# A new order table for the engines of an attention and feed-forward kernel

## The chip, the cores and the metric

The kernel runs on one core of a Trainium2 chip. A core has four engines that compute, each with its own list of instructions that it works off in order: TensorE (PE in the profile; its weight loads are PEld), VectorE (DVE), ScalarE (ACT) and GpSimd (POOL). SyncE (SP) only issues transfers. The metric is device microseconds (us) of one execution, as the median of several runs.

## The reference

Two layers in a row. The first is attention through 32 memory slots per head, for 8 batches, 8 heads, 576 tokens, 64 elements per head. The second is a feed-forward layer on 4608 tokens, 512 wide inside and outside and 2048 wide in the middle:

```
a      = softmax(phi, over tokens)               # 8 x 8 x 576 x 32
k_m    = a^T k ;  v_m = a^T v                    # 32 x 64 per head
attn   = softmax(q k_m^T / 8, over the 32 slots)
x      = attn v_m, heads side by side            # 4608 x 512
h      = x w_in                                  # 4608 x 2048
out    = (h * cos(h)) w_out                      # 4608 x 512
```

All inputs and outputs are fp32, but for w_in and w_out, which arrive as 64-bit floats and are brought to fp32 on the chip.

## The kernel before

**The work.** x is never formed. As x w_in = attn (v_m w_in), the kernel multiplies the 32 x 64 memories of a batch by w_in (a *fold*: tiles pv and vw, lines 641 to 687), and the attention weights aT by that (first product, tile hp, line 718). For batch 0 and 1 a fold is in fp32 (line 659, tiles pvf and pv), for the later ones in pairs of fp16 numbers (lines 645 and 650). hp is turned into h cos(h) by six steps that alternate between ScalarE and VectorE: lines 729 (ACT), 730 (DVE), 735 (ACT, Sin), 739 (DVE), 741 (ACT) and 742 (DVE); the result is gp, again a pair of fp16 numbers. The second product (line 760) multiplies gp by w_out (tile wo) into acc. In group 0 both products are fp32 (lines 709 and 755), and gp ends at line 737.

**Tiling.** The 4608 rows are 12 groups of 384, a group has three acc tiles of 128 rows, and 16 steps f over the middle dimension: 192 steps (grp, f) in all. While group 0 runs, the eight parts of w_in and the eight of w_out are loaded into three buffers (raw0 to raw2, `load_w_in` and `load_w_out`), brought to fp32 (`to_float32`: cast line 257, shift and or line 260, Square line 263, whose end frees the buffer), and split into fp16 pairs in group 1 (lines 303 to 315). The memories of a batch (psA, line 460), its scores (sc, line 562) and its folds are made some way ahead of the groups that use them.

**Tile sizes on TensorE.** A matmul uses the 128 x 128 array whole (lines 709, 718, 755, 760, 812), or a part: 128 x 32 (most of line 460, and line 645) or 64 x 32 (lines 562, 650, 659). Small matmuls on different parts can run beside each other. An fp32 product is two hardware matmuls in the trace, so a fold at line 659, written as 8 matmuls, is 16 of the trace.

**Buffers.** Three banks hold hp, two hold small results (pv, psA, sc and others in turn), three hold acc.

**The order.** The program is written as loops that emit all instructions in a program order. Then `issue_in_order` (last line of `attention_then_ffn`) sets, for every engine, the order in which it issues them, from the table `NEXT`. A word of the table is a position in what is left of the engine's program-order list, and `xN` repeats it: `0x26` takes the first one 26 times, `8` takes the one that then stands eight places behind the front. An engine waits at an instruction until its operands are there, and all behind it waits too. The waits themselves follow from the data, whatever the order. 43 matmuls of zeros (line 812, "warm") fill TensorE's time while the first inputs arrive.

Of the kernel before, what the change touches and what calls it, by code (L numbers as in the profile page):

```python
# [49 lines left out]
        "0x16 2x2 0x16 1x8 0x10 1x8 0 1x8 0x8 1 0x2 1 0x50 2 3 4 5 0x4 8 0x2 7 8 0x6 5x2 0x2 1 0x2 16x2 26x2 "  # L50
        "0 79 65x2 77 1 0x6 70 0 1 2 0x3 1 0x3 80 79 58 0 1 2 3 54 0x4 66 67 66 0x40 34x3 36x2 34 0x2 32x2 0 "
        "1 0x4 1 0 24x2 0x8 18 19 0x2 27 1 0 1 0 1 0 10 8x2 16x2 0x3 1 0 1 0x2 8x2 18 16x2 17 16 18x2 16x2 "
        "0x6 1 0 11 8 0x2 1 0 1 0x2 1x3 0x5 1 0x4 2x2 0x2 4 0x4 1x2 0 1 0 14 1x13 0 22 0x2 1 0x4 1 0 27 0x12 "
        "2x12 1 2x13 0x4 13x3 0 12x3 0x12 3x2 4 5 3x2 4 3x16 0x3 6x12 3x3 9x3 0x3 24x3 0x3 15x3 0x3 12x3 0x24 "
        "6x3 0x7 19x3 1 0x2 1 0x15 6x12 0x3 6x3 0x3 6x12 0x3 3x3 0x3 18x3 3x3 18x3 0x30 3x3 6x12 9x3 0x6 3x3 "
        "0x3 20x3 0x14 3x3 0x3 40x5 0x41 6x3 0x3 3 0x5 8x3 0x12 1 2 0 2 0x9 17x6 6x4 7 6x2 7 8 6x2 3x3 0x9 "
        "3x6 12x6 3x3 0x6 6x3 0x3 3x3 15x3 12x2 73x2 0x3 9 0x6 12x6 0x3 6x3 15x6 0x6 6x3 0x6 12x3 6x6 0x18 "
        "9x3 0x9 3x3 0x12 3x3 0x13 1 0 1 0 1 0 40x9 0x40 8x6 3x5 20x6 0x3 6x3 3x3 0x7 1 0 1 0x4 3x3 17x3 3 4 "
        "5 3 5 3x3 0x3 9x3 0x6 3x4 27x3 0x8 1 2 3 0x4 6x3 0x6 9x3 0x3 6x3 15x3 0x15 3x9 0x6 6x8 0x3 3 4 3 4 5 "
        "3 14x3 5x9 0x3 11 0x5 6x8 0x6 6x3 18x3 6x6 0x27 1 0x2 1 2 0x8 6x3 0x3 3x6 9x3 3x3 0x12 3x3 0x3 3x10 "  # L60
        "4 3 4 5 3x8 6x3 3x3 0x3 3x6 0x3 6x3 3x3 12x3 3x6 0x3 15x3 3x3 15x9 16 17 15x2 16 15x2 3x6 9x12 0x3 "
        "3x3 0x24 3x6 0x21 15x3 0x3 18x8 0x12 14x15 6 7 6x2 7 6x3 0x6 46x12 0x3 43x3 0x3 46x15 43x3 40x3 0x40 "
        "8x7 13x3 6 7x5 0x6 1x3 0 27 3x4 7 8 9 10 0x11 8x11 0 1 2 3 4x3 0x4 3x3 29x3 3 4 3 4 3x2 4 3x13 0x3 "
        "3x3 21x3 18x3 3x12 0x3 18x3 0x15 21x3 6x12 0x3 3x3 0x3 18x3 3x12 0x3 3x3 0x3 18x3 0x15 3x15 0x3 3x3 "
        "0x9 3x3 0x3 9x3 21x3 0x3 6x6 12x3 0x6 18x3 6x3 0x6 6x3 0x18 28x3 0x3 3x9 4 3 4 3 4 3x2 0x3 9x3 21x3 "
        "6x3 0x15 3x9 0x3 3x9 0x20 1 2 0 2 0x2 1 0 6x3 9x3 0x9 12x3 9x3 0x6 12x3 3x6 0x3 6x6 3x3 0x3 9x8 3x3 "
        "6x3 7 6 7 6x2 0x3 43x6 54x6 0x3 43x3 0x43 5x2 12x3 6x3 9 5 3x2 8x3 0x6 5x3 0x5 14x3 0x2 1 2 0x2 1 "
        "0x7 3x11 0x5 1 0 1 0x3 8x9 0 1 2 3 0x4 3x9 9x9 0x6 3x3 6x3 0x15 12x2 0x3 10x3 0x9 1x3 0x10 6x6 3x3 "
        "0x6 3x3 0 14x3 8x3 0x8 3x6 0x3 6x3 3x3 15x3 0x9 3x9 0x3 3x3 0x3 3x8 4 3 4 3 4 3x9 0x6 3x3 9x3 45x4 "
        "3x6 15x3 0x18 9x3 3x9 0x3 3x6 4 3x5 0x3 18x3 0x12 3x15 0x3 9x12 3x3 0x3 6x3 3x3 0x6 12x3 0x26 1 2 "  # L70
        "0x2 1 0x3 12x6 0x15 40x12 46x3 40x3 55x3 40x15 0x43 5x15 3x5 6x4 10 11 12 13 0x6 16 0x8 8x14 11x3 0 "
        "1 2 3 0x7 26x3 0x2 1 0x3 1 0 12x3 27x3 0x15 15x3 0x15 12x9 0x27 3x3 0x3 18x3 0x12 3x3 0x3 15x6 0x15 "
        "96x4 12x9 0x18 3x12 0x3 3x3 15x3 0x3 9x3 42x4 0x9 3x9 0x3 3x3 0x3 6x3 0x9 3x2 4 3x5 0x3 12x3 0x6 6x6 "
        "0x3 3x3 39x4 9x6 18x6 0x6 6x3 0x6 24x6 6x3 0x6 3x5 4 5 3x5 0x3 3x3 0x3 3x6 0x3 3x3 6x6 3x3 0x3 6x3 "
        "0x3 18x8 9x3 12x3 0x3 63x3 9 10 9 10 9x4 0x49 20x2 9x3 0x6 5x6 12x3 0x3 6x3 3x6 9x3 0x10 1 2 0x3 1 "
        "0x7 24 0x8 1 2 3 0 3 0x2 17x2 0 8x5 12x3 8x3 0x2 1 2 0x2 1 0x2 9x3 6x3 0x18 6x9 3x3 6x3 0x6 6x3 18x2 "
        "6x3 16x3 15 6x3 0x12 9x4 3x6 0x3 11x3 0x2 21x3 9x3 0x9 9x3 0x3 39x8 0x9 9x3 6x6 12x3 15x3 0x6 23x3 "
        "9x2 10 9 10 11 9x2 0x6 21x3 12x3 0x9 3x6 15x3 0x9 9x3 0x6 15x3 9x3 0x3 9x13 10 9x2 0x6 3x12 0x6 3x3 "
        "0x3 15x6 12x3 27x3 0x12 33x3 0x12 3x3 0x3 12x3 46x3 12x3 0x28 12x3 0x15 12x6 0x12 15x3 33x3 15x3 "
        "30x3 0x3 12x3 58x3 0x24 31x3 0x13 1 0 1 0x3 30x3 27x3 0x12 30x3 3x12 0x6 15x3 12x3 24x3 42x3 0x12 "  # L80
        "12x3 27x3 0x15 27x3 0x12 33x3 0x15 3x3 18x3 3x12 24x3 0x6 30x3 0x15 9x3 3x6 18x3 0x18 12x3 24x3 6x3 "
        "33x3 0x6 9x3 0x3 6x3 24x3 0x12 12x3 21x3 33x3 12x3 6x12 30x3 6x6 12x3 6x9 24x3 6x6 9x3 18x3 0x3 3x9 "
        "18x3 30x3 6x6 3x3 6x3 30x3 15x3 24x3 3x3 33x3 9x3 3x12 15x3 3x3 0x3 21x3 0x6 12x3 0x18 3x3 0x3 6x3 "
        "0x3 9x3 3x3 0x3 3x3 0x9 3x6 9x3 6x3 0x9 "),
    mybir.EngineType.Activation: (
# [897 lines left out]
```

## Time and profile before

| | |
|---|---|
| median of 3 runs | 691.31 us (691.0 to 692.96) |
| the profiled execution's own time | 690.88 us |
| its span, first to last instruction | 689.1 us |
| TensorE busy | 676.9 us (98%) |
| VectorE busy | 524.1 us (76%) |
| ScalarE busy | 499.3 us (72%) |
| mean granted TensorE clock | 0.997 |

The span lies inside the execution's time; 1.8 us lie around it. Matmuls are pipelined and their ends in the trace are modelled: a matmul's duration runs on while the next has started, and "busy" is the union of these. What a stretch of TensorE work costs is therefore read from the starts of its rows. In the timeline a row is one or more like instructions: start, length, engine, line, operation, tiles, form and count; what stands in brackets is the engine's idle time before it, and what ended that.

### The profile page before, as it was taken

What the parts mean: (1) busy time and instruction counts of PE and PEld (TensorE: products, weight loads), DVE (VectorE), ACT (ScalarE), POOL (GpSimd) and SP (SyncE); (2) the same over time, 40 slices, a digit from 0 to 9 for tenths busy, and PEclk for the clock granted to TensorE, in tenths of its full rate; (3) what the DMA queues carried; (4) which work ended last, traced back from release to release, by engine and by line L of the source; (5) the groups of instructions that cost most, each with busy time, mean ns of one, the idle gap of its engine ahead of it and who ended that gap; (6) DMA issues with size and microseconds to landing.
All of it is one profiled execution on the core that took longest, in us unless ns stands there. A gap on an engine that the chain in (4) does not pass through costs nothing.

```text
span 689.1 us, 12262 instructions
## 1 busy us (share of the span) xinstructions
PE 676.9 (98%) x4815; PEld 346.7 (50%) x4815; DVE 524.1 (76%) x1117; ACT 499.3 (72%) x934; POOL 20.0 (3%) x26
## 2 busy tenths in 40 slices
PE   8899999999999999999999999999999999999997
PEld 3343446564554445555444445655445445665553
DVE  6789999999879765797668965798657876566643
ACT  2698999988788865779665965778746856665653
POOL 4020000000000000000000000000000000000000
PEclk9999999999999999999999999999999999999999
DMA  8997784337043000620105300350100000100001
GB/s 294 381 336 260 296 267 120 87 70 265 16 148 111 31 1 1 217 73 0 47 2 174 114 1 1 116 174 0 47 1 2 15 32 1 47 1 1 16 30 47
DMA packets 28521, 66.21 MB, mean 96 GB/s; under 512 B 2288, under 2 KB 12400, under 8 KB 26416
## 3 DMA queue, kind: packets, MB, share of 16 engines
q1 hardware_dynamic: 24000, 57.43, 25.2%
q10 hardware_dynamic: 4464, 8.00, 3.1%
q8 instruction: 38, 0.62, 0.4%
q14 instruction: 19, 0.16, 0.1%
HBM read 51.79 MB, written 9.44 MB: 89 GB/s over the span
## 4 chain that ended last, share of the span: by engine, by line
PE 87%; DVE 5%; ACT 3%; DMA 2%; issue 1%; SPq 0%; ACTq 0%
PE acc L760 46%; PE hp L718 24%; PE acc L755 5%; PE hp L709 3%; PE psA L460 3%; PE pv L645 2%; DMA raw_in<-in_w_in 2%; PE sc L562 1%; PE pv L650 1%; PE pvf L659 1%; DVE u L730 1%; DMA kv<-in_k_first 1%; ACT gp L729 1%; DVE u L739 1%; PE pv L659 1%
## 5 line engine op out<-in xcount | busy, mean ns | idle before, releaser
L760 PE MATMUL acc<-wo,gp 128*128 128x512 f16 x1584 | 373.4, 379 | 0.2 <-ACT gp L741 0.2
L760 PEld LDWEIGHTS <-gp 128*128 128x128 f16 x1584 | 151.1, 98 | 168.2 <-issue 11.5
L718 PE MATMUL hp<-aT,vw 128*128 128x192 f16 (+1 forms) x1440 | 199.1, 284 | 0.9 <-DVE u L739 0.5
L718 PEld LDWEIGHTS <-vw 128*128 128x128 f16 x1440 | 129.0, 98 | 71.6 <-issue 10.9
L729 ACT ACTIVATE gp<-hp,cu 128x192 int32<-128x192 f32 (+1 forms) x240 | 114.4, 490 | 48.8 <-PE hp L718 32.9
L730 DVE SCALAR_TENSOR_TENSOR u<-hp,cu,gp 128x192 f32<-128x192 f32 (+1 forms) x240 | 117.8, 502 | 40.5 <-ACT gp L729 39.6
L735 ACT ACTIVATE u<-u,quarter 128x384 f32<-128x384 f32 x192 | 115.7, 612 | 44.3 <-DVE u L730 42.7
L739 DVE SCALAR_TENSOR_TENSOR u<-hp,u 128x384 f32<-128x384 f32 x176 | 96.2, 552 | 46.7 <-ACT u L735 45.9
L742 DVE TENSOR_TENSOR gp<-u,gp 128x384 f16<-128x384 f32 x176 | 96.0, 551 | 31.5 <-ACT gp L741 30.5
L741 ACT CAST gp<-u 128x384 f16<-128x384 f32 x176 | 87.9, 507 | 38.4 <-DVE u L739 35.7
L755 PE MATMUL acc<-wo,gp 128*128 128x512 f32 x96 | 46.6, 605 | 0.2 <-DVE gp L737 0.2
L666 DVE SCALAR_TENSOR_TENSOR vw<-pv,vw 128x512 f16<-128x512 f32 x48 | 32.3, 684 | 14.2 <-ACT vw L665 14.2
L665 ACT ACTIVATE vw<-pv 128x512 f16<-128x512 f32 x48 | 27.1, 591 | 8.6 <-PE pv L650 8.4
L755 PEld LDWEIGHTS acc<-wo,gp 128*128 128x128 f32 x96 | 16.9, 190 | 18.8 <-issue 15.2
L784 ACT ACTIVATE ob<-acc,os 128x512 f32<-128x512 f32 x27 | 18.2, 686 | 11.2 <-PE acc L760 10.4
L709 PE MATMUL hp<-aT,vf 128*128 128x384 f32 x64 | 24.2, 499 | 0.2 <-DVE gp L737 0.2
L735 ACT ACT_TABLE_LOAD x17 | 21.8, 1283 | 0.3
L460 PE MATMUL psA<-kv,phi 128*32 128x129 f32 (+1 forms) x560 | 17.8, 275 | 0.0
L709 PEld LDWEIGHTS hp<-aT,vf 128*128 128x128 f32 x64 | 11.5, 189 | 12.2 <-issue 4.8
L460 PEld LDWEIGHTS psA<-kv,phi 128*32 128x32 f32 (+1 forms) x560 | 14.5, 109 | 4.1 <-issue 2.2
L562 PE MATMUL sc<-q,km 64*32 64x288 f32 (+2 forms) x256 | 14.1, 414 | 1.2 <-DVE om L795 0.5
L812 PE MATMUL warm<-zeros 128*128 128x512 f16 x43 | 14.0, 468 | 1.2 <-DVE vmask L173 1.2
(157 smaller groups left out, 486.4 us busy)
## 6 DMA issues: line engine op xcount, KB each, us to landing
kv<-in_kv SPq DMA_DIRECT2D x28, 516.0 KB, 6.4
raw_out<-in_w_out SPq DMA_DIRECT2D x8, 1024.0 KB, 6.4
q<-in_qT SPq DMA_DIRECT2D x7, 1152.0 KB, 5.6
out<-ob ACTq DMA_DIRECT2D x30, 256.0 KB, 2.1
raw_in<-in_w_in SPq DMA_DIRECT2D x6, 1024.0 KB, 7.9
phi<-in_phi SPq DMA_DIRECT2D x8, 512.0 KB, 5.7
w_in_sb<-w_in_parts SPq DMA_DIRECT2D x12, 256.0 KB, 4.3
wo<-in_w_in SPq DMA_DIRECT2D x2, 1024.0 KB, 13.9
```

What stands on the lines that cost most here:

```text
L460: nc.tensor.matmul(psA[32 * j:32 * (j + 1), g * KV:(g + 1) * KV], lhsT=a[:n, c, h * M:(h + 1) * M], rhs=kvs[c][:n, h * KV:(h + 1) * KV], s ...
L666: nc.vector.scalar_tensor_tensor(out=vw[:, 1, g], in0=src, scalar=T, in1=vw[:, 0, g], op0=ALU.mult, op1=ALU.subtract)
L709: nc.tensor.matmul(hp[:, :GT], lhsT=st["vf", q][:, g, fo * P:(fo + 1) * P], rhs=st["aTf"][:, g], start=(g == 0), stop=(g == 1))
L718: nc.tensor.matmul(hp[:, c0:c0 + n], lhsT=vw[:, wi, g, fo * P:(fo + 1) * P], rhs=aT[:, ai, g, c1:c1 + n], start=(k == 0), stop=(k == 5))
L729: nc.scalar.activation(ni[:, c], hp[:, c], AF.Copy, scale=cu, bias=0.25)
L730: nc.vector.scalar_tensor_tensor(out=u[:, c], in0=hp[:, c], scalar=cu, in1=ni[:, c], op0=ALU.mult, op1=ALU.subtract)
L735: nc.scalar.activation(u, u, AF.Sin, scale=TWO_PI_BELOW, bias=quarter)
L739: nc.vector.scalar_tensor_tensor(out=u, in0=hp[:, :GT], scalar=2.0 ** -17, in1=u, op0=ALU.mult, op1=ALU.mult)
L741: nc.scalar.copy(gp[:, 0], u)
L742: nc.vector.tensor_tensor(out=gp[:, 1], in0=u, in1=gp[:, 0], op=ALU.subtract)
L755: nc.tensor.matmul(accs[grp][t], lhsT=gp[:, t * P:(t + 1) * P], rhs=wo[:, f + 1], start=(f == 0), stop=(f == NF - 1))
L760: nc.tensor.matmul(accs[grp][t], lhsT=gp[:, gi, t * P:(t + 1) * P], rhs=parts[:, wi], start=(f == 0 and gi == 0 and wi == 0), stop=(f == N ...
```

## The change

Only the table `NEXT` is changed. The instructions, their operands and their number are the same (4143 matmuls as written, 915 instructions of ScalarE, 1117 of VectorE, 22 of POOL, 112 of SP); SP's list is the same word for word. 3828, 838, 1079 and 11 of the first four stand at another place of their engine's list, half of TensorE's by 9 places or fewer. The diff, cut to the first lines of each engine:

```diff
 NEXT = {
     mybir.EngineType.PE: (
-        "0x16 2x2 0x16 1x8 0x10 1x8 0 1x8 0x8 1 0x2 1 0x50 2 3 4 5 0x4 8 0x2 7 8 0x6 5x2 0x2 1 0x2 16x2 26x2 "
-        "0 79 65x2 77 1 0x6 70 0 1 2 0x3 1 0x3 80 79 58 0 1 2 3 54 0x4 66 67 66 0x40 34x3 36x2 34 0x2 32x2 0 "
...
+        "0x26 8 0x16 1x8 2x8 0 2x8 5x3 0x2 4 5 3x2 4 3x2 7x24 9x16 0x3 6x2 8 9 10 0x4 4x2 5 4x2 0x4 6 7 8 6x3 "
+        "0x6 1 0x3 16 27x2 16 0 1 2 0x5 72 58x2 0 1 2 0x3 1 0 62 60 0x2 59 58 74x2 75 0 1 2 3 0x4 67 0x40 "
...
     mybir.EngineType.Activation: (
-        "0x6 4 0 3 0x4 2 3 0 1 5 8 1 9 12 4 8 1 0 8 4 2 0 9 1 8 2 10 0x2 3 0 12 2 15 5 10 0x3 10 0 3 6 1 5 0 "
...
+        "0x4 1x3 3x2 1x2 0 1 4 2x2 6 0 2 4 9 12 6 8 10 1 4 12 3 1 3 13x2 3 0 16 5 2 18 2x2 3 2 14 10 0 1 0x2 "
...
     mybir.EngineType.DVE: (
-        "0 5 0 5 4 0 1 2x2 1x7 0x5 1 0x4 6x3 0 5 0x2 7 3 0 2 1x2 0x2 1 2 0x2 1 0 13 15 11 15 11 0 19 1 0 17 0 "
...
+        "0 7 8x3 0 7x9 5 6 7x2 13 2 12 5 4 10x2 14 9x3 4 8x6 3 8 7 18 1 18 6 16 7 19 25 17 18 15x2 6 20 6x2 "
...
     mybir.EngineType.Pool: (
-        "0x22 "),
+        "2 0 3 2 1 0 1x2 0x5 1 0x8 "),
     mybir.EngineType.SP: (
         "0x35 5 0x3 2 0x13 12 1 0x8 1 0x2 2x2 0x6 2x2 0x6 2x2 0x6 2x2 0x6 2x2 0x12 "),
 }
```

What the unrolled lists hold for TensorE, where a *run* is a stretch of small tiles between two whole ones, and a *piece* is a stretch of one line's matmuls:

| | before | after |
|---|---|---|
| changes of tile size, whole list | 199 | 167 |
| changes of tile size from the first pvf_2 product on | 179 | 148 |
| runs of small tiles from there on | 77 | 58 |
| of these psA (line 460) | 7 | 7 |
| sc (line 562) | 16 | 15 |
| pvf and pv in fp32 (line 659), 10 folds | 15 | 10 |
| pv in fp16 pairs (lines 645 and 650), 24 folds | 39 | 26 |
| pieces of line 645, and of line 650 | 30, 28 | 26, 26 |
| runs that end in an fp32 tile of line 709 or 755 | 16 | 12 |

On POOL the clearings of w_in_sb and wo come in another order, and the first two clearings of wo by line 270 stand ahead of the first all-reduce (l3_0), behind which they stood. On VectorE two of the three clearings of w_in_sb (line 189) stand behind the start of the first batch's maximum, and the use of l3_0 (line 277) stands later.

148 rows, old and new, of the table NEXT are left out of this document.

## Prediction

> **What bounds the kernel now.** I read the page first: its busy line, then the chain of waits, then the costliest group.
>
> ```profile
> span 689.1 us, 12262 instructions
> PE 676.9 (98%) x4815; PEld 346.7 (50%) x4815; DVE 524.1 (76%) x1117; ACT 499.3 (72%) x934; POOL 20.0 (3%) x26
> ...
> PE 87%; DVE 5%; ACT 3%; DMA 2%; issue 1%; SPq 0%; ACTq 0%
> ...
> L760 PE MATMUL acc<-wo,gp 128*128 128x512 f16 x1584 | 373.4, 379 | 0.2 <-ACT gp L741 0.2
> ```
>
> TensorE is busy nearly throughout and makes up 87% of the chain. The mean of 379 ns is a duration from start to modelled end, and matmuls overlap; what one costs the stream is the distance between starts. For that I read TensorE's timeline (first number: start; second: duration).
>
> ```profile
> 208.25 0.71 PE L562 MATMUL sc<-q,km 64*32 64x288 f32 x16
> 208.90 1.47 PE L760 MATMUL acc<-wo,gp 128*128 128x512 f16 x6
> 210.21 1.14 PE L718 MATMUL hp<-aT,vw 128*128 128x384 f16 x6
> 211.27 0.40 PE L645 MATMUL pv<-w_in_sb,vp 128*32 128x512 f16 x4
> 211.60 1.47 PE L760 MATMUL acc<-wo,gp 128*128 128x512 f16 x6
> 213.00 0.40 PE L645 MATMUL pv<-w_in_sb,vp 128*32 128x512 f16 x4
> 213.33 0.41 PE L650 MATMUL pv<-w_in_sb,vl 64*32 64x512 f16 x8
> 213.68 0.82 PE L760 MATMUL acc<-wo,gp 128*128 128x512 f16 x3
> 214.33 1.14 PE L718 MATMUL hp<-aT,vw 128*128 128x384 f16 x6
> 215.31 2.75 PE L760 MATMUL acc<-wo,gp 128*128 128x512 f16 x12
> 217.90 1.14 PE L718 MATMUL hp<-aT,vw 128*128 128x384 f16 x6
> ```
>
> Twelve L760 matmuls take 217.90 - 215.31 = 2.59 us, 0.216 each. Six that are followed by a small tile take 213.00 - 211.60 = 1.40, where 6 x 0.216 is 1.30: **entering a small tile size costs 0.10 us**. The stream shows no gap here, and still time goes: into entering small tiles, and into short pieces of small tiles, which cost almost as much as long ones (below).
>
> Then the busy time by stage: startup, group 0, group 1, groups 2 to 10 (columns: length; busy time of PE, PEld, DVE, ACT, POOL; clock; DMA). The bounds are the first L755 or L760 matmul of each group.
>
> ```profile
> 0.00:33.40 33.40, 27.61 (x275) 11.13 (x275) 22.85 (x48) 13.49 (x23) 8.51 (x11) 0.95 0.96 335
> 33.40:111.70 78.30, 77.44 (x455) 35.49 (x456) 71.49 (x151) 73.16 (x123) 4.66 (x5) 1.00 0.77 269
> 111.70:169.40 57.70, 57.44 (x474) 32.67 (x473) 54.67 (x119) 52.32 (x105) 0.35 (x1) 1.00 0.50 138
> 169.40:640.20 470.80, 469.15 (x3387) 245.24 (x3385) 350.06 (x755) 335.46 (x641) 6.45 (x9) 1.00 0.16 52
> ```
>
> TensorE's idle time after 33.4 us is 0.86 + 0.26 + 1.65 = 2.8 us. So from group 0 on the end is set by how much stream time TensorE's own list takes. But in groups 0 and 1 VectorE and ScalarE are nearly full too: VectorE idles 6.8 + 3.0 = 9.8 us of 136, ScalarE 5.1 + 5.4. There a worse order of theirs would show at once. From 169 us on they have a quarter of the time free.
>
> **The change part by part.** No instruction is added or removed; Sin and Exp alternate equally often in both ScalarE lists, so the activation table loads stay 34. SP's list is the same. I unrolled both lists of each engine and compared.
>
> *TensorE, from the first pvf_2 product on.* The same 161 instructions stand ahead of that point in both lists, so the rest is the same work: 179 changes of tile size before, 148 after; 77 runs of small tiles before, 58 after. Prices of pieces, from starts again:
>
> ```profile
> 41.60 0.81 PE L709 MATMUL hp<-aT,vf 128*128 128x384 f32 x2
> 42.34 0.64 PE L659 MATMUL pvf<-w_in_sb,vm 64*32 64x256 f32 x8
> 42.91 0.91 PE L709 MATMUL hp<-aT,vf 128*128 128x384 f32 x2
> ...
> 82.16 0.62 PE L659 MATMUL pvf<-w_in_sb,vm 64*32 64x256 f32 x2
> 82.71 1.12 PE L755 MATMUL acc<-wo,gp 128*128 128x512 f32 x2
> ...
> 128.82 1.04 PE L659 MATMUL pv<-w_in_sb,vm 64*32 64x512 f32 x2
> 129.79 0.82 PE L760 MATMUL acc<-wo,gp 128*128 128x512 f16 x3
> ...
> 271.01 0.61 PE L645 MATMUL pv<-w_in_sb,vp 128*32 128x512 f16 x8
> 271.56 2.15 PE L718 MATMUL hp<-aT,vw 128*128 128x192 f16 x24
> ```
>
> - L659 with 256 columns: two hardware matmuls (one fp32 product) hold the stream 0.55 us, eight hold it 0.57. A piece costs 0.55 whatever is in it. Pieces 10 to 6: 4 x 0.55 = **2.2 us**.
> - L659 with 512 columns: one product alone holds 0.97. Pieces 5 to 4: **1.0 us**.
> - L645 and L650, the 24 folds: four L645 hold 0.33 and eight hold 0.55, so a fold cut in two pays 2 x 0.33 - 0.55 = 0.11; the L650 part holds 213.68 - 213.33 = 0.35. Pieces of L645 30 to 26: 4 x 0.11 = 0.4; of L650 28 to 26: 2 x 0.35 = 0.7. **1.1 us**.
> - L562: 16 runs become 15. A whole set holds 0.65. The row of a half was not free of waits, so I bound it: a half cannot cost less than half a set (saving 0) nor more than a whole (saving 0.65). I take 0.6, since in the nearest rows, L659's, a piece costs nearly the whole.
> - Entering: 19 runs fewer x 0.10 = **1.9 us**.
> - Leaving into an fp32 tile: two L709 hold 41.60 to 42.34, drawn with 0.81, but 0.91 behind pvf: 0.10 more. Such exits 16 to 12: **0.4 us**.
>
> Sum: 2.2 + 1.0 + 1.1 + 0.6 + 1.9 + 0.4 = **7.2 us** of stream taken off. In this measure gp_1_15's first use, near the end of group 1, comes 3.7 us earlier.
>
> [...]
>
> *TensorE's first 161 instructions (startup).* The warm matmuls stand as 14, 2, 7, 1, 2, 3, 4, 4, 6 in place of 14, 8, 2, 1, 4, 4, 2, 2, 6, and VectorE does one clearing of w_in_sb ahead of the maximum and two later, in place of three early. TensorE idles 5.8 us in this stage and the clock mean of 0.95 is worth 0.05 x 33.4 = 1.7 us. What sets this stage are loads and conversions in a chain; SP issues the same loads in the same order. Bounds: a gain of 1.7 if the slow stretch of clock goes away, a loss of 1.7 if a second one comes. I take 0, as both lists reach gp_0_0 with nearly the same VectorE work ahead of it (22.7 and 22.0 us).
>
> *VectorE and ScalarE in groups 0 and 1.* Here a loss could hide. For every gp tile I added up the durations of all VectorE instructions that stand in its list ahead of the tile's last step (L737 or L742), and the stream time of all TensorE instructions ahead of its first use, in both lists. The margin after is the margin seen now, less the VectorE work put ahead, plus the TensorE work put ahead. The largest shift is at gp_1_0:
>
> ```profile
> 103.73 0.55 DVE L742 TENSOR_TENSOR gp<-u,gp 128x384 f16<-128x384 f32 x1
> ...
> 111.65 0.81 PE L760 MATMUL acc<-wo,gp 128*128 128x512 f16 x3
> ```
>
> Now it is ready at 104.28 and used at 111.65: 7.4 us. VectorE's list has 5.5 us more ahead of it, TensorE's 0.6 less: 1.3 left. Over the 32 tiles of both groups none falls below zero; the least is 0.6 (gp_1_8). This holds if VectorE idles no more than its present 9.8 us. The same sum for vf, vw and the converted weights gives 0.7 or more wherever groups 0 and 1 read them. In groups 3 to 10 the TensorE work between an hp tile and its gp's first use has a shortest value of 8.9 us, where it was 6.3, so waits there should not grow. New waits net of old ones: from -2.8 (all present idle goes) to +9.8 (VectorE's idle doubles and all of it lands); I take **+1.1**, the idle that TensorE shows in groups 0 and 1 now, once more.
>
> *POOL.* The all-reduce for l3_0 moves behind two clearings of wo that wait for ScalarE. Its reader on VectorE moves back by more (from 16.0 to 56.5 us of VectorE work), so nobody stands behind it: 0. If VectorE came early it would wait for ScalarE's Squares of parts 2 and 3 of w_in, within the +9.8.
>
> *The tail.* Both lists end with acc_11_2's matmuls and the same evacuation: 0, or some tenths more since acc_11_0 and acc_11_1 end nearer to the end.
>
> Sum against the profiled execution's own 690.88 us: 690.88 - 7.2 + 1.1 = 684.8. The median of the runs, 691.31, lies 0.43 above that execution, so I forecast **685.2 us** for a median.
>
> **The rivals.**
> - *VectorE and ScalarE cap groups 0 and 1.* TensorE's 3.7 us there turn into waits: 685.2 + 3.7 = 688.9. For it: 6.8 and 3.0 us of idle only. Against: the margins stay positive.
> - *A late weight load.* ScalarE's Square frees the buffer of raw_out_0 for the load of raw_in_4.
>
> ```profile
> 37.61 1.06 ACT L263 ACTIVATE raw_out<-wo 128x1024 f32<-128x1024 f32 x1
> ...
> 54.85 1.35 ACT L257 CAST w_in_sb<-raw_in 128x1024 f16<-128x1024 bf16 x1
> DMA to landing us min/median/max: 4.8/7.9/12.3
> ```
>
>  Of the 16 us between them 14.9 are ScalarE work now, 6.8 in the new list, less than the median landing of raw_in (7.9; the last row, from the view of that tile). At worst 12.3 - 6.8 = 5.5 us late on a nearly full engine: 690.7. Against: seven other such pairs stand only 5.8 to 7.9 us of ScalarE work apart now.
> - *The pieces filled idle time*, so that the change doesn't shorten what matters: 691. Against: the stream shows 2.8 us of idle, less than 7.2.
> - *Slower.* VectorE's list stands in worse step with ScalarE's in groups 0 and 1, each waiting for the other in order, and its idle doubles by 9.8 us. Past the margin at gp_1_0 each us of it delays TensorE: 685.2 + 9.8 - 1.3 = 693.7. It outweighs the gain from some 8 us of extra idle on. For it: 93% full, and an order made with mean durations.
> - *TensorE has room after all.* If its matmuls could follow each other faster than the list shows, it would be held by others and a shorter list would change nothing: 691.3. Twelve in 2.59 us without a gap speak against it. [...]
>
> **How the numbers follow.** Some 0.3% (2.1 us) is what a measurement of this kernel can tell from no change. The forecast (682.3 to 688): 0.67. VectorE's cap 0.12, half of it beyond 689.2; late load 0.05, two fifths faster; idle filled 0.08, same; slower 0.07; TensorE with room 0.01, same. Faster 0.67 + 0.06 + 0.02 = 0.75; same 0.06 + 0.03 + 0.08 + 0.01 = 0.18; slower 0.07. The range goes from 682.3 (the old waits gone too) to 690.5, which takes in the cap and most of the late load.
>
> **What would show it.** Right: folds as L645 x8 and L650 x8 in one piece, about 0.89 us from start to the next large tile; L659 in whole groups; the first L755 at 33 +- 2 us; gaps of TensorE after it of some 4 us at the most; first use of gp_2_0 2 to 3 us earlier than 169.4. Wrong: idle of TensorE that ends on L737, L742 or L666 in groups 0 and 1, VectorE idling over 12 us there, or ScalarE waiting for raw_in between 45 and 60 us.

## The result, and the profile after

The changed kernel takes 684.97 us (median of 5 runs, 684.13 to 687.55) where the kernel before takes 691.31 (690.64 to 692.96): a ratio of 0.9912 with a 95% interval of 0.9886 to 0.9937. The forecast was 685.2 us, in a range of 682.3 to 690.5. The profiled execution took 684.29 us.

Lines of the changed kernel stand 4 further down: L764 is the old L760, L759 the old L755, L722 the old L718, L663 the old L659, L649 and L654 the old L645 and L650. In the kernels of the experiments the lines are shifted by a few in the same way; the tiles tell which is meant. First the page: busy line, chain, costliest group.

```profile
span 682.5 us, 12301 instructions
PE 670.8 (98%) x4815; PEld 347.3 (51%) x4815; DVE 518.7 (76%) x1117; ACT 494.1 (72%) x934; POOL 20.7 (3%) x26
...
PE 74%; DVE 11%; ACT 10%; DMA 2%; issue 2%; SPq 0%; ACTq 0%; DVEq 0%
...
L764 PE MATMUL acc<-wo,gp 128*128 128x512 f16 x1584 | 373.4, 379 | 0.3 <-DVE gp L746 0.2
```

The counts of the engines' own work and the mean of 379 ns are the old ones. What is new is the chain: TensorE 74% where it was 87%, VectorE and ScalarE 21% where they were 8%. More of the end now hangs on a tile that TensorE takes up the moment it is ready. The stages, in the same bounds of time as before:

```profile
0.00:33.40 33.40, 27.78 (x291) 11.88 (x292) 23.01 (x43) 12.90 (x21) 8.16 (x10) 1.00 0.96 336
33.40:111.70 78.30, 78.30 (x490) 37.90 (x489) 74.16 (x161) 77.19 (x135) 5.95 (x6) 1.00 0.78 268
111.70:169.40 57.70, 57.70 (x458) 32.99 (x457) 55.03 (x119) 52.81 (x102) 0.35 (x1) 1.00 0.28 69
169.40:640.20 470.80, 468.38 (x3389) 245.72 (x3388) 346.87 (x758) 331.83 (x643) 6.23 (x9) 1.00 0.18 60
```

Three things are to be seen. The clock of the startup is 1.00 where it was 0.95. Between 33.4 and 169.4 us TensorE has no idle time at all (1.1 us before), VectorE has 6.8 us (9.8 before) and ScalarE 6.0 (10.5). The changed kernel does some of group 2 in this time; in its own groups 0 and 1, from 32.79 to 161.94 us, VectorE idles 6.4 us and ScalarE 5.8. Behind 169.4 TensorE idles 2.4 us, more than the 1.65 of before. The folds and their surroundings on TensorE's timeline:

```profile
32.19 0.67 PE L663 MATMUL pvf<-w_in_sb,vm 64*32 64x256 f32 x16
32.79 1.12 PE L759 MATMUL acc<-wo,gp 128*128 128x512 f32 x2
...
208.93 0.61 PE L649 MATMUL pv<-w_in_sb,vp 128*32 128x512 f16 x8
209.48 0.41 PE L654 MATMUL pv<-w_in_sb,vl 64*32 64x512 f16 x8
209.82 2.76 PE L764 MATMUL acc<-wo,gp 128*128 128x512 f16 x12
212.42 1.14 PE L722 MATMUL hp<-aT,vw 128*128 128x384 f16 x6
```

A fold stands in one piece and takes 209.82 - 208.93 = 0.89 us. Twelve output matmuls still take 2.60 us, 0.216 each.

The profiled executions differ by 6.59 us: the first output matmul starts 0.64 us earlier (32.79 for 33.43), from there to the last matmul's end it is 646.04 us where it was 652.02 (5.98 less), and the rest up to the end of the span is the same (3.67 for 3.66).

This last measure, **from the first output matmul to the last matmul's end**, is used in all that follows. It is much sharper than the run's time: in two executions of the changed kernel the starts of the output matmuls, counted from the first one, agreed within 0.03 us at each of 27 places over the 646 us. It is still one execution, and one accident has to be known. At 330 us of the kernel before, ScalarE issues two output transfers, which took 1.46 us; in e_warm_before, whose lists are the same there, they took 0.92:

```profile
329.74 1.46 ACTq L786 DMA_DIRECT2D out<-ob  x2
...
334.46 1.63 PE L760 MATMUL acc<-wo,gp 128*128 128x512 f16 x6 [0.15 <-ACT gp L741]
```

```profile
330.26 0.92 ACTq L781 DMA_DIRECT2D out<-ob  x2
```

The first rows are of the kernel before, the last of e_warm_before. ScalarE's next steps came later for it, gp_5_2 was late, and the output matmuls waited 0.47 us at 334 us; e_warm_before has no wait there and is 0.45 us shorter at just this place. So some 0.45 of the 5.98 us belongs to that execution and not to the order. The table below is worked out from the starts of TensorE's matmuls. "Runs" are stretches of small tiles behind 32 us and "their time" goes from their start to the next large tile. "Waits" are distances between large matmuls beyond 0.216, 0.163 and 0.083 us (512, 384 and 192 columns in 16 bits), 0.429, 0.323 and 0.110 (fp32; 512, 384 and 128 columns), and 0.093 more into a small tile, each where it is over 15 ns.

```
kernel         runs  their time  waits 32-170  waits behind 170  first output to last  median of the runs (kernel before beside it)
before          77      63.9         3.2            2.5               652.0             691.31
after           58      59.0         1.5            4.9               646.0             684.97  (691.31)
after_again     58      59.0         1.5            4.9               646.0             684.26  (691.99)
e_join          56      64.3         6.5            2.6               653.0             692.85  (692.27)
e_join_late     64      63.2         3.5            3.4               650.8             691.44  (691.99)
e_cutB          78      65.5         1.7            5.0               654.7             693.94  (692.27)
e_cutAB         78      60.2         2.0            5.8               650.5             690.21  (692.27)
e_start         58      59.0         3.1            5.0               646.2             687.36  (692.27)
e_pool          57      58.7         1.5            4.9               646.4             684.43  (691.99)
e_repair        58      59.2         1.5            5.5               646.9             686.82  (691.99)
e_warm          58      59.0         1.7            4.9               646.1             684.19  (692.06)
e_warm_before   77      63.9         3.5            2.1               651.6             690.24  (692.06)
e_best          56      59.0         1.5            5.0               645.8             684.48  (692.06)
e_swap          58      59.0         1.5            4.2               645.4             683.44  (692.30)
```

The measured 5.98 us are the 4.9 of the shorter runs and 1.8 for 19 entries at 0.093, less 0.7 of new waits. Most of it comes early. Both lists have the same large matmuls ahead of the first use of gp_3_0, and there (222.77 us before, 216.96 after) the changed kernel is already 5.2 us ahead, counted from the first output matmul. Behind it the runs of small tiles go on to get shorter, but new waits of 2.0 us leave only 0.8.

### The profile page after: what moved, and what is told of

Read it like the earlier page. It is cut to its first block, busy times and chain, and to the rows that moved or that the text cites. A ratio compares the mean times of both kernels' runs of the same rounds, so it can differ in the third digit from the quotient of the medians.

```text
span 682.5 us, 12301 instructions
## 1 busy us (share of the span) xinstructions
PE 670.8 (98%) x4815; PEld 347.3 (51%) x4815; DVE 518.7 (76%) x1117; ACT 494.1 (72%) x934; POOL 20.7 (3%) x26
## 4 chain that ended last, share of the span: by engine, by line
PE 74%; DVE 11%; ACT 10%; DMA 2%; issue 2%; SPq 0%; ACTq 0%; DVEq 0%
PE acc L764 37%; PE hp L722 19%; PE acc L759 6%; PE hp L713 3%; DVE u L734 2%; ACT u L739 2%; PE psA L464 2%; ACT gp L733 2%; DVE u L743 2%; DVE gp L746 2%; DMA kv<-in_v_first 1%; PE pv L649 1%; ACT gp L745 1%; PE sc L566 1%; PE pv L654 1%
## 5 line engine op out<-in xcount | busy, mean ns | idle before, releaser
L764 PE MATMUL acc<-wo,gp 128*128 128x512 f16 x1584 | 373.4, 379 | 0.3 <-DVE gp L746 0.2
L764 PEld LDWEIGHTS <-gp 128*128 128x128 f16 x1584 | 151.1, 98 | 169.5 <-issue 11.3
L722 PE MATMUL hp<-aT,vw 128*128 128x192 f16 (+1 forms) x1440 | 199.9, 283 | 1.7 <-DVE u L743 0.8
L722 PEld LDWEIGHTS <-vw 128*128 128x128 f16 x1440 | 130.0, 98 | 73.6 <-issue 10.0
L733 ACT ACTIVATE gp<-hp,cu 128x192 int32<-128x192 f32 (+1 forms) x240 | 115.8, 492 | 68.0 <-PE hp L722 36.1
L759 PE MATMUL acc<-wo,gp 128*128 128x512 f32 x96 | 45.9, 604 | 0.0
L759 PEld LDWEIGHTS acc<-wo,gp 128*128 128x128 f32 x96 | 16.9, 190 | 19.0 <-issue 16.9
L713 PE MATMUL hp<-aT,vf 128*128 128x384 f32 x64 | 22.7, 491 | 0.0
L464 PE MATMUL psA<-kv,phi 128*32 128x129 f32 (+1 forms) x560 | 17.9, 275 | 0.1
L572 DVE STREAM_TRANSPOSE at<-sc 128x288 f32<-128x288 f32 (+2 forms) x32 | 14.2, 464 | 1.2 <-PE sc L566 1.2
```

The lines of the kernel that those rows point to most:

```text
L464: nc.tensor.matmul(psA[32 * j:32 * (j + 1), g * KV:(g + 1) * KV], lhsT=a[:n, c, h * M:(h + 1) * M], rhs=kvs[c][:n, h * KV:(h + 1) * KV], s ...
L713: nc.tensor.matmul(hp[:, :GT], lhsT=st["vf", q][:, g, fo * P:(fo + 1) * P], rhs=st["aTf"][:, g], start=(g == 0), stop=(g == 1))
L722: nc.tensor.matmul(hp[:, c0:c0 + n], lhsT=vw[:, wi, g, fo * P:(fo + 1) * P], rhs=aT[:, ai, g, c1:c1 + n], start=(k == 0), stop=(k == 5))
L733: nc.scalar.activation(ni[:, c], hp[:, c], AF.Copy, scale=cu, bias=0.25)
L759: nc.tensor.matmul(accs[grp][t], lhsT=gp[:, t * P:(t + 1) * P], rhs=wo[:, f + 1], start=(f == 0), stop=(f == NF - 1))
L764: nc.tensor.matmul(accs[grp][t], lhsT=gp[:, gi, t * P:(t + 1) * P], rhs=parts[:, wi], start=(f == 0 and gi == 0 and wi == 0), stop=(f == N ...
```

## The experiments

All the edits are edits of the order lists, apart from the added warm-up matmuls. They are shown in the unrolled list of one engine: line, tile, and number of instructions in a row.

### What a cut costs in the changed kernel: e_cutB and e_cutAB

In 20 folds of the changed list three of the large matmuls that follow are put into the fold (output matmuls in 14 of them, hidden ones, those of hp, in 6): in e_cutB into the middle of its L654 part, in e_cutAB between its two parts. This is the fold of 2_0:

```diff
 L649 pv_2_0 x8
+L764 acc_2_2 x3      (e_cutAB)
 L654 pv_2_0 x4
+L764 acc_2_2 x3      (e_cutB)
 L654 pv_2_0 x4
-L764 acc_2_2 x3
 L764 acc_2_0 x3
```

> The changed kernel, and in each of the 20 folds whose L645 and L650 matmuls stand in one run, the eight L650 matmuls are cut into four and four, with the three large matmuls that follow put between them. Nothing else moves. Theory: each place pays one more L650 piece (0.33) and one more entry (0.10), 20 x 0.43 = 8.6 us: 685.0 + 8.6 = 693.6. Rival (TensorE's stream is not the limit): under 687.

> The changed kernel, and in each of the same 20 folds the three large matmuls that follow are put between the eight L645 and the eight L650 matmuls: one change of tile size more at each place, and no piece more. Theory: 20 x 0.10 = 2.0 us: 687.0. Rival (a change of tile size is free and only short pieces cost): 685.0.

Measured: e_cutB 693.94 us (692.25 to 696.65; ratio to the kernel before 1.0034, 1.0017 to 1.005) and e_cutAB 690.21 (687.28 to 692.49; 0.9968, 0.9953 to 0.9984). In the sharp measure e_cutB is 8.7 us above the changed kernel and e_cutAB 4.5. TensorE's timeline of e_cutB:

```profile
211.64 0.40 PE L650 MATMUL pv<-w_in_sb,vl 64*32 64x512 f16 x4
211.97 0.82 PE L760 MATMUL acc<-wo,gp 128*128 128x512 f16 x3
212.72 0.40 PE L650 MATMUL pv<-w_in_sb,vl 64*32 64x512 f16 x4
213.05 2.12 PE L760 MATMUL acc<-wo,gp 128*128 128x512 f16 x9
```

and of e_cutAB:

```profile
211.38 0.62 PE L645 MATMUL pv<-w_in_sb,vp 128*32 128x512 f16 x8
211.93 0.82 PE L760 MATMUL acc<-wo,gp 128*128 128x512 f16 x3
212.69 0.41 PE L650 MATMUL pv<-w_in_sb,vl 64*32 64x512 f16 x8
213.03 2.12 PE L760 MATMUL acc<-wo,gp 128*128 128x512 f16 x9
```

Four L650 hold 0.33 us where eight hold 0.34, and three output matmuls ahead of a small tile hold 0.75 where 3 x 0.216 is 0.65. So a cut into L650 costs 0.33 + 0.10 = 0.43 us, 20 of them 8.6 us, and that is what came. A cut between the parts should cost the entry alone, 0.10 x 20 = 2 us. The kernel lost 4.5, and its median lies 3.2 us above the 687.0 expected: the rest is new waits, 1.4 us between large tiles and 1.2 us inside runs of small ones. So the prices of the prediction hold where they can be read off rows. In the changed table nothing hides them, and more can come on top.

### The pieces of the old table put together: e_join and e_join_late

The reverse in the kernel before: TensorE's list alone is changed, and all 19 sets that stand in two or three pieces are put in one, at the place of the last piece or, where the lists would then wait for each other in a ring, of the first. The other engines keep their old lists. One of the 19:

```diff
 L709 hp_0_2 x2
-L659 pvf_2 x1
 L755 acc_0_0 x1
 L709 hp_0_3 x2
 L755 acc_0_1 x1
-L659 pvf_2 x7
+L659 pvf_2 x8
 L755 acc_0_2 x1
```

> The kernel before with TensorE's list alone changed: every split set of small matmuls after the first pvf_2 product (19 of 49 sets: lines 659, 645 with 650, and 562) is put into one piece, at the place of its last part (one set, the fold of batch 2 and quarter 2, at the place of its first). All other lists are those of before. Changes of tile size from that point on 179 to 143, runs of small tiles 77 to 56. Theory (TensorE's stream sets the end and pays per piece and per entry): pieces of line 659 15 to 10 (4 x 0.55 + 0.97 = 3.2), of line 645 30 to 24 (6 x 0.11 = 0.7), of line 650 28 to 24 (4 x 0.35 = 1.4), sc 0.6, entries 21 x 0.1 = 2.1, exits into fp32 0.3: 8.3 us less, so 683.0, or up to 687 if the folds that now end no earlier but begin later make ScalarE and VectorE wait in their unchanged lists. Rival (the gain comes from the better lists of ScalarE and VectorE, and the pieces filled time that TensorE had to wait anyway): 691, or slower than that.

Measured: 692.85 us (692.34 to 695.06), 1.0014 times the kernel before (1.0002 to 1.0025): the rival. In the sharp measure it is 653.0 us, 1.0 more than before. There are 21 runs fewer, and they take as long as the 77 did. The reason stands in TensorE's timeline. The kernel before, at the fold 3_3 and the scores of group 4:

```profile
288.35 0.40 PE L645 MATMUL pv<-w_in_sb,vp 128*32 128x512 f16 x4
288.68 0.40 PE L650 MATMUL pv<-w_in_sb,vl 64*32 64x512 f16 x4
289.01 0.82 PE L760 MATMUL acc<-wo,gp 128*128 128x512 f16 x3
289.91 0.40 PE L645 MATMUL pv<-w_in_sb,vp 128*32 128x512 f16 x4
290.24 0.40 PE L650 MATMUL pv<-w_in_sb,vl 64*32 64x512 f16 x4
...
292.17 0.69 PE L562 MATMUL sc<-q,km 64*32 64x288 f32 x8 [0.53 <-DVE om L795]
292.79 0.82 PE L760 MATMUL acc<-wo,gp 128*128 128x512 f16 x3
293.84 0.69 PE L562 MATMUL sc<-q,km 64*32 64x288 f32 x8 [0.22 <-DVE at L568]
```

and e_join (its lines stand 5 higher):

```profile
84.87 1.04 PE L654 MATMUL pv<-w_in_sb,vm 64*32 64x512 f32 x2
86.79 1.09 PE L654 MATMUL pv<-w_in_sb,vm 64*32 64x512 f32 x14 [0.88 <-DVE m_in L290]
...
292.13 0.40 PE L640 MATMUL pv<-w_in_sb,vp 128*32 128x512 f16 x4
293.04 0.40 PE L640 MATMUL pv<-w_in_sb,vp 128*32 128x512 f16 x4 [0.51 <-DVE vm L482]
293.37 0.41 PE L645 MATMUL pv<-w_in_sb,vl 64*32 64x512 f16 x8
...
295.37 0.69 PE L557 MATMUL sc<-q,km 64*32 64x288 f32 x8
296.98 0.69 PE L557 MATMUL sc<-q,km 64*32 64x288 f32 x8 [0.91 <-DVE at L563]
```

In the old list the output matmuls between the two halves of a set ran while VectorE emptied the small-result bank that the second half is written to (for the fold by the copies `vm`, which read tpx there, for the scores by the transposes `at`). Put together, the second half of the fold waits 0.51 us and that of the scores 0.91. At 84.87 a set of 512 columns starts its second product 1.9 us after its first; in the kernel before the whole set took 1.01 us (83.77 to 84.78). So many of the old pieces stood where TensorE would have waited anyway; the saving on pieces came back as waits.

e_join_late joins only 11 of the 19 sets, those behind which e_join showed no such wait.

```diff
 L645 pv_4_2 x8
-(large tiles between)
 L650 pv_4_2 x8
+(the large tiles, moved ahead of the set)
```

> The kernel before, with TensorE's list changed alone: 11 of the 19 fold sets that stand in two or three pieces are put in one piece, those of groups 2_1, 2_2, 3_2, 4_2, 4_3, 5_1, 6_0 to 6_3 and 7_0; the sets of groups 0 and 1, the two sets that end a group's folds (3_3 and 5_3) and the scores of group 4 stay split, since TensorE waited in or behind those when all 19 were joined (1.9 us inside one of 256 columns, 3.4 us in the scores behind 3_3 and 5_3). Tile-size changes 179 to 160, small-tile runs 77 to 64. Price theory (a piece costs its measured 0.32 to 0.55 us and an entry 0.093 us wherever no wait stands): three sets of 4 + 12 at 0.20, one of 8 + 6 + 2 at 0.51, five of 8 + 8 at 0.09, one of 4 + 4 + 8 at 0.30, one of 15 + 1 at 0.40, in all 2.3 us less from the first output matmul to the last: 649.7 us there instead of 652.0, and about 690.0 in the median. Rival (in this table the pieces filled time in which TensorE would wait for ScalarE and VectorE, as in the run with all 19 joined): no gain, 652 us from the first output matmul to the last and 692 in the median.

Measured: 691.44 us (689.72 to 692.39; ratio 0.9992, 0.9982 to 1.0002), which is no change that can be told, and 650.8 us in the sharp measure: 1.2 us less, half of the 2.3. Of this 1.2 the late transfer of the kernel before, which this execution doesn't have, makes some 0.4: against e_warm_before it is 0.8. Waits behind 170 us grew by 0.9. So even among sets chosen for having no wait only a third to a half of the price is paid out. TensorE's new list with the other engines' old lists, and the reverse, can't be run: in both, engines wait for each other in a ring and none goes on.

### The startup: e_start and e_pool

e_start is the changed kernel with TensorE's first 161 instructions in the order of before; e_pool the changed kernel with POOL's old list.

```diff
 (TensorE, e_start)
-L816 warm 14, 2, 7, 1, 2, 3, 4, 4, 6 between the others
+L816 warm 14, 8, 2, 1, 4, 4, 2, 2, 6 between the others
 (POOL, e_pool)
-L189 w_in_sb x2, L190 wo, L189 w_in_sb x3, L270 wo x2, L425 l3_0
+L189 w_in_sb x5, L190 wo, L425 l3_0, L270 wo x2
```

> The changed kernel with TensorE's first 161 instructions in the order of before (the same 161, among them the 43 warm matmuls); all else is the changed table. Theory (the startup gave only the 0.6 us by which the first L755 came earlier in the changed kernel's profile): 685.6. Rival (the order of the warm matmuls keeps the clock up, and that is a good part of the gain): 687 or more, with a granted clock under 1.0 in every run.

> The changed kernel with POOL's old list, so that of the change only TensorE's, ScalarE's, VectorE's and SyncE's lists are left. Theory: POOL's list is worth nothing, as the prediction put it: within 0.7 us of the changed kernel at the same clock, and from the first output matmul to the last 646.0 us. Rival: POOL's new order of its five weight DMAs is what brings the first output matmul 0.6 us earlier, which would start at 33.4 us or later here, and the median is 0.6 us or more above the changed kernel.

POOL's list has no transfers; what the expectation calls weight DMAs are clearings.

Measured: e_pool 684.43 us (684.04 to 686.54) with the first output matmul at 32.23 and 646.4 us from there; POOL's list is worth nothing, as forecast. e_start 687.36 us (687.08 to 687.68; ratio 0.9934, 0.9919 to 0.9948), with all four runs at a clock of 0.994 or 0.995: the rival. From the first output matmul on it is the changed kernel (646.2), but that matmul starts at 35.90 where the changed kernel has 32.79. TensorE's timeline of e_start:

```profile
35.30 0.67 PE L658 MATMUL pvf<-w_in_sb,vm 64*32 64x256 f32 x16 [1.44 <-DVE w_in_sb L259]
35.90 1.12 PE L754 MATMUL acc<-wo,gp 128*128 128x512 f32 x2
```

The fold ahead of the first output matmul waits 1.44 us for VectorE's part of w_in_sb, and 21.3 to 28.1 us ran at half clock. This part of w_in_sb comes later because VectorE's list has it behind the copies of the first two folds (vf, line 681 there). These waited 1.27 and 1.83 us for TensorE and started at 26.46 and 31.18 us, where they start at 24.73 and 28.07 in the changed kernel. So TensorE's delay comes back to it through VectorE's list. How much of it is the half clock and how much the order itself isn't separated.

### The clock of the startup: after_again, e_warm and e_warm_before

The runs of the changed kernel spread over 3 us, and the time goes with the mean clock.

> The changed kernel itself once more, on the chip of this call, in many runs, as the reference for the other three and for how its runs spread. Theory (the order lists alone set the time, and what a run adds is a stretch of halved TensorE clock in the startup, of 0 to 6.8 us as the profiles so far show, which costs half its length): runs of 684.2 us at a clock of 1.000 and about 687.5 at 0.990, median 685 to 686, and about 7 us under the kernel before at the same clock. Rival (the first five runs were lucky): a median above 687.

Measured: 684.26 us (683.61 to 686.64; ratio 0.9903, 0.9882 to 0.9923), under the 685 to 686 expected. Over its ten runs those at a clock of 0.996 or more took 683.61 to 684.97 us, those at 0.995 took 686.27 to 686.64, the one at 0.989 took 687.55. The kernel before reached 1.000 in 1 of its 63 runs beside the experiments. Where the clock falls, the stage view shows. Its first columns are the stretch, its length and TensorE's busy time; the clock stands behind POOL. The kernel before:

```profile
19.60:23.00 3.40, 0.86 (x6) 0.43 (x10) 2.29 (x7) 3.12 (x6) 0.35 (x1) 1.00 1.05 393
23.00:26.40 3.40, 3.40 (x26) 0.64 (x19) 2.54 (x6) 1.44 (x4) 0.00 (x0) 0.50 1.01 414
```

The changed kernel in the execution of after_again:

```profile
11.90:15.30 3.40, 2.08 (x22) 0.79 (x22) 1.66 (x6) 0.27 (x1) 0.00 (x0) 1.00 1.03 399
15.30:18.75 3.45, 3.45 (x72) 1.65 (x74) 2.57 (x5) 0.00 (x0) 0.00 (x0) 0.51 1.06 347
```

and in the execution of the first profile:

```profile
17.10:20.50 3.40, 2.15 (x67) 1.28 (x67) 3.28 (x5) 0.36 (x2) 0.00 (x0) 1.00 0.97 340
20.50:23.90 3.40, 2.26 (x16) 0.75 (x14) 2.43 (x5) 2.87 (x6) 0.00 (x0) 1.00 1.06 412
```

In the kernel before a stretch in which TensorE is busy 0.86 of 3.40 us (25%) is followed by one at half clock, and in after_again one with 2.08 (61%). In the first profile of the changed kernel stretches of 2.15 and 2.26 (63 and 66%) are not. The stretches are laid in steps of 3.4 us, the length of the one at half clock in the kernel before (23.0 to 26.4 us), from the place where the clock first rises. In the kernel before the warm matmuls start 0.43 us apart up to 5.9 us, and 0.216 apart behind it; the fall at 23.0 lies 17.1 us further on, five times the 3.41 of that stretch. In the first profile of the changed kernel the rise lies at 6.9 us. That the busy share of these stretches decides is the author's reading, which no run shows alone: in e_start a stretch with the same 2.15 of 3.40 us (17.9 to 21.3 us) is followed by half clock. A stretch at half clock did not show in the time of after_again: its execution, with one at 15.30 to 18.75 us, has its first output matmul at 32.64 us, where the first profile, at full clock, has 32.79 and waits 1.8 us for the load of v. The profiles of e_cutB and e_start, with a mean clock of 0.995, have two such stretches in a row (19.7 to 26.5 and 21.3 to 28.1 us), and the runs of the changed kernel at 0.995 are those that took 2 us longer. The test was to fill the gaps with matmuls on zeros:

```diff
     fold_first(0)
-    warm(6)
+    warm(17)
 (TensorE's list, e_warm)
+L816 warm x3
 L395 tpx_k x2
+L816 warm x1
 L566 sc_0_0 x1
...
 L375 psv x8
+L816 warm x2
 L375 psv x8
+L816 warm x1
...
+L816 warm x1, and x3 seven instructions on
 L663 pvf_0_0
 (TensorE's list, e_warm_before)
+L812 warm x2
 L411 tpx_v x1
+L812 warm x3
 L411 tpx_v x1
+L812 warm x6
 L659 pvf_0_0
```

> The changed kernel with 11 more warm-up matmuls of 128x512 on zeros, put into the gaps of its startup in which TensorE waits: three ahead of the transposes of k at 13 us, one ahead of the first scores at 14, three among the matmuls of v's memory at 17 to 18, one and three ahead of the first folds at 21.5 and 24. Theory of the clock (the ten profiles so far: a stretch of 3.4 us, counted from the first rise of the clock, in which TensorE was busy for 61% or less is followed by a stretch at half clock, seven of seven; with 65% or more none of them is; 63 and 64% went both ways): no stretch of the startup falls under 65% any more, whatever the phase, so that every run has a clock of 1.000, the runs lie within 0.6 us, and the median is 684.0 to 684.6. Rival (the clock falls for another reason, such as the other engines' or the DMAs' load, or the added matmuls come in the way of the first folds): runs of 0.995 and 0.997 as before, spread over 2 us or more, or a median of 685 or more with a clock of 1.000.

> The kernel before with 11 more warm-up matmuls in the gaps of its startup: two and three ahead of the two transposes of v at 19.4 and 20.2 us, six ahead of the first fold at 21.3 (1.5 us of waiting there). Theory of the clock: in the kernel before these gaps lie within 3.4 us of one another (2.7 us idle in all), so that nearly any phase has a stretch under 65% busy: 39 of its 40 runs had a clock under 1.000. Filled, the clock stays at 1.000 and the time falls by half of the 3.4 to 6.8 us that ran at half clock, 1.0 to 2 us: a median of 690.0 to 690.8 where the kernel before has 692. Then some 1 us of what the change brought in the median is the clock, through the shorter gaps of its startup, and about 6 us the rest. Rival: within 0.4 us of the kernel before, with clocks of 0.995 to 0.998 as there.

Measured: e_warm_before 690.24 us (689.55 to 690.94), 0.9969 times the kernel before (0.9958 to 0.9981), with clocks of 0.997 to 1.000 (ten of eleven at 0.999 or 1.000). So the kernel before gains 1.8 us in the median with its gaps filled and its clock up. The 0.4 by which it is shorter in the sharp measure (651.6 for 652.0) is the late transfer at 330 us in the profile of the kernel before, and no part of this gain. e_warm: 684.19 us (683.92 to 685.41), all clocks 0.999 or 1.000. The clock came as forecast; the spread did not shrink to 0.6 us, because one run at full clock took 685.41: its first output matmul started at 33.85, and its longest wait for the load of v was 1.1 us, where the first profile of the changed kernel has 0.8. The two filled kernels, at full clock but for one run of e_warm_before (0.997, the profiled one), are 6.05 us apart in the median and 5.5 in the sharp measure.

### The late waits: e_repair, e_best and e_swap

The changed kernel's waits behind 170 us are new. The waits of TensorE there, by line (total, times, longest), and of its weight loads for gp, first in the changed kernel and then in the one before:

```profile
PE hp L722 <- DVE u L743: 0.8, 4, 0.3
PE hp L722 <- DVE vw L670: 0.5, 1, 0.5
PE acc L764 <- DVE gp L746: 0.2, 1, 0.2
...
PEld L764 <- DVE gp L746: 3.9, 9, 0.7
```

```profile
PEld L760 <- DVE gp L742: 1.0, 4, 0.5
```

These rows show only the part of a wait that no drawn duration covers. By the starts, 3.2 of the table's 4.9 us stand ahead of hidden matmuls (12 places; for u or vw where a row names the tile) and 1.3 ahead of output matmuls (7 places; for gp). In the kernel before it was 1.0 (2 places) and 0.5 (2 places, both behind the late transfer).

e_repair puts, at 14 places, the waiting matmuls behind the next ones of the other kind, as at 240 us:

```diff
+L764 acc_3_1 <- gp_3_5 x3
 L722 hp_3_12 x6
-L764 acc_3_1 <- gp_3_5 x3
```

> The changed kernel with 14 swaps in TensorE's list behind 200 us: where TensorE waited over 0.13 us between large matmuls (hidden matmuls on their buffer or on a folded weight, or output matmuls on a gate product just made), the waiting three or six matmuls are put behind the next three or six of the other kind. The waits at these places are 4.0 us in all. Theory (the changed table gave back 2.4 us in late waits, and these are a matter of order only): 2 to 4 us less, since part of the swapped-in matmuls will wait too: 682.5 us in the median where the changed kernel has 685.5, and large-tile waits behind 170 us under 3 us instead of 4.9. Rival (VectorE or ScalarE is the bound there, and TensorE only waits elsewhere): within 0.7 us of the changed kernel, waits of 4.5 us or more at other places.

Measured: 686.82 us (685.13 to 686.97; four of the five runs at a clock of 0.995), and 646.9 us in the sharp measure, 0.8 more than the changed kernel; waits behind 170 us 5.5. That is the rival's side, and a little worse than it said. The starts of the output matmuls tell the swaps apart: those at 221, 240, 269, 378 and 600 us brought 0.8 us together, the pair at 314 and 318 lost 1.6, the rest nothing. The pair's place:

```profile
314.42 2.11 PE L717 MATMUL hp<-aT,vw 128*128 128x384 f16 x12
318.76 1.14 PE L717 MATMUL hp<-aT,vw 128*128 128x384 f16 x6 [2.23 <-DVE u L738]
```

The swaps put three hidden tiles in a row, and the third waits 2.23 us until VectorE has emptied a buffer. e_best takes the five good swaps, the 11 warm-up matmuls, and puts the two sets that still stood in two pieces, 6_0 and 7_0, in one:

```diff
-L649 pv_6_0 x8
 (66 other instructions)
+L649 pv_6_0 x8
 L654 pv_6_0 x8
```

> The changed kernel with the 11 warm-up matmuls, with the five of the 14 swaps that brought something by the times of the single output matmuls (at 221, 240, 269, 378 and 600 us: 0.8 us in all; the two at 314 and 318 together lost 1.6, the rest nothing), and with its two fold sets that still stood in two pieces, 6_0 and 7_0, in one (0.2 us). Theory: 645.0 us from the first output matmul to the last (646.0 in the changed kernel), and a median of 683.0 to 683.6. Rival (waits of ScalarE and VectorE take the swaps' place when they are combined): 645.7 us or more.

Measured: 684.48 us (684.24 to 684.61) and 645.8: the rival's number, but not for its reason. At 480 us the first half of fold 6_0, gone from where it stood, leaves TensorE a wait of 0.43 us on u, as the timeline of e_best shows:

```profile
480.07 1.14 PE L718 MATMUL hp<-aT,vw 128*128 128x384 f16 x6 [0.43 <-DVE u L739]
```

e_swap is e_best without this join:

> The changed kernel with the 11 warm-up matmuls and the five swaps, but with sets 6_0 and 7_0 left in two pieces, since putting 6_0 in one piece moved its first half 14 us later and the hidden matmuls at 479 us waited 0.6 us there. Theory: 645.3 us from the first output matmul to the last (645.85 with the joined sets, of which the join lost 0.46), every clock 0.999 or 1.000, and a median of 683.6 to 684.1. Rival (the loss at 479 us comes from the swaps before it): 645.8 us again.

Measured: 683.44 us (682.91 to 683.83; ratio to the kernel before 0.9873, 0.9849 to 0.9897), all clocks 0.999 or 1.000, and 645.4 us in the sharp measure, as expected; the median is 0.2 us under the range. Its timeline at the same place:

```profile
479.01 0.61 PE L645 MATMUL pv<-w_in,vp 128*32 128x512 f16 x8
479.56 1.15 PE L718 MATMUL hp<-aT,vw 128*128 128x384 f16 x6
```

The first half of fold 6_0 fills just the time in which u is made. e_swap is the fastest kernel of this study. Its gain over the changed kernel is 0.7 us in the sharp measure and some 0.8 us against the median of 684.26 of after_again, too little to tell from the medians alone.

## Why the prediction was right, and where it was not

- **TensorE's stream, 7.2 us less: right in size.** The runs of small tiles take 4.9 us less (63.9 to 59.0) and 19 entries fewer are 1.8 us at 0.093, together 6.7. The fp32 exits, priced at 0.4, are among the waits of the table: 15 of 0.10 us before and 12 after, 0.3 less. That makes 7.0. The cuts in the changed table measure the two prices a second time.
- **"TensorE has room after all": fell.** Twelve output matmuls still take 2.60 us, 0.216 each (2.59 before), and the median is 684.97 where the rival had 691.3.
- **"The pieces filled idle time": right about TensorE's list alone, wrong about the change.** The prediction argued against this rival that the stream shows 2.8 us of idle, less than 7.2. That step is wrong. Time that pieces fill is no longer shown as idle: e_join took them away, and at once there were 3.4 us more of waits between large tiles, and waits of 0.5 to 1.9 us inside the joined sets. The gain needs the other engines' lists too. That the new lists of VectorE and ScalarE bring it fits the changed kernel's stages: no TensorE idle in groups 0 and 1, and 3.4 and 4.7 us less idle on those two engines in its own groups 0 and 1. It is not shown by a run, since TensorE's list and the others' can't be exchanged one without the other.
- **New waits, net 1.1 us: right in size, wrong in place.** By the table's measure waits went from 5.7 to 6.4 us, 0.7 more, or 1.0 without the fp32 exits. In groups 0 and 1, where the prediction put them, they fell by 1.7. In the later groups they grew by 2.4, where it said that "waits there should not grow" because the shortest distance from a hidden tile to its product's use had risen. The step failed twice. The larger part are hidden matmuls that wait for their buffer (u) or for a folded weight (vw), 2.2 us more than before, which the prediction had not added up there. And the distance itself was no guard: output matmuls wait 0.9 us more for gp though the shortest distance had risen; TensorE's work between the two doesn't tell when ScalarE and VectorE get to the tile.
- **VectorE idles no more than 9.8 us in groups 0 and 1: right,** 6.4. The margins came out smaller than the sum, though: gp_1_0, which moved most, was ready at 106.86 us and first used at 107.03, 0.2 us for the 1.3 forecast. "Slower" and "VectorE and ScalarE cap groups 0 and 1" fall with it.
- **A late weight load: didn't come.** In the changed kernel the loads of raw_in land in 4.9 to 7.0 us, and between 40 and 75 us ScalarE and VectorE wait at most 0.6 us around that tile.
- **First use of gp_2_0 2 to 3 us earlier: too little.** It came at 161.9 us, 7.5 us earlier. Of this 0.6 us are the startup, 0.9 large matmuls that the new list puts behind it, and some 1.7 the waits of groups 0 and 1 that went away where 1.1 more had been forecast; the rest is mainly shorter runs of small tiles.
- **POOL and the tail, 0: right** (e_pool; 3.67 us behind the last matmul for 3.66).
- **The startup, 0: wrong, within its bounds of 1.7 either way.** The slow stretch of clock went away in the profiled execution, and the first output matmul came 0.64 us earlier. In the medians the startup's share is larger: at full clock the two kernels are 6.05 us apart (e_warm, e_warm_before), and the medians of the kernel before and the changed one were 6.3 and 7.7 us apart in the two comparisons. The step that failed is "what sets this stage are loads and conversions in a chain": the order of TensorE's first 161 instructions matters too. With the old order all four runs of e_start had a clock of 0.994 or 0.995, where six of the changed kernel's ten had 0.996 to 1.000; and with 11 more warm-up matmuls in the gaps the kernel before had 0.999 or 1.000 in ten of eleven runs.

So 685.2 was near because the terms were the right ones for the two tables together; two of their places, and the reason given against one rival, were not. That it came within 0.2 us of the median is luck: the changed kernel's own two medians are 0.7 us apart, the startup gave some tenths that the forecast had at 0, and 0.45 us of the measured stream is the late transfer in the profile of the kernel before.

## What to carry to other kernels

Before a short piece of work is joined to its other half, look at what that half would then wait for: the price of the piece can be read off starts (here 0.10 us for an entry and 0.33 to 0.97 for the piece), but taken away in one engine's list alone it came back as waits, since a timeline doesn't show as idle the waits that are filled with work. A reordering is priced by the distances of every operand and every buffer, not of one kind. Where two kernels differ by tenths of a per cent, compare the starts of one recurring instruction in the two traces, counted from its first; two executions of one kernel agreed within 0.03 us so, where medians resolve 1 to 2. A step at a single place has to be looked up all the same: one late transfer made 0.45 us.

## What the runs showed of the hardware

- Half clock came behind a stretch of 3.40 us in which TensorE was busy 0.86 us (25%, the kernel before), 1.50 (44%, e_warm_before), 2.08 (61%, after_again and e_cutB) or 2.15 (63%, e_start). By the author's windows on their profiles the shares were 29% in e_join, 42% in e_join_late and 61% in e_cutAB and e_repair. Full clock stayed behind 2.15 and 2.26 us (63 and 66%, first profile of the changed kernel), behind 2.56 of 3.50 and of 3.40 (73 and 75%, e_warm), and, by the same windows, behind 51% in e_start and 53% in e_pool (mean clock 1.000), both the first stretch behind the clock's rise. So the 65% in the expectations of e_warm and e_warm_before is a line that the author drew between shares; what decides isn't shown.
- In the kernel before the half clock ended behind a stretch busy throughout (3.40 of 3.40 us). In e_start and e_cutB a second half-clock stretch followed a first with 2.71 and 3.05 of 3.40 (80 and 90%).
- In after_again and e_cutB 1.32 us of idle time in one stretch of 3.40 us (3.40 - 2.08) was enough; in the first profile of the changed kernel 1.25 was not.
- Behind the first output matmul, two executions of the changed kernel agreed to 0.03 us over 646 us. Issuing an output transfer from ScalarE is one thing that varies: two issues took 1.46 us in one execution and 0.92 in another, and 0.45 us of this reached TensorE.
